# Placing the weight looks by the one plan, and storing the last output tile in two transfers

## The chip, the cores and the metric

The kernel runs on one core of one Trainium2 chip. The metric is the time of one execution on the device in microseconds (us). TensorE multiplies matrices and leaves sums in PSUM banks of 128 partitions by 512 float32. VectorE and ScalarE read those banks and write to on-chip memory (SBUF). GpSimd makes masks. SyncE issues the transfers (DMA). Each engine works through its own instruction list in order and waits on semaphores for the others.

## The reference

Attention with a decaying state (per head 48 wide, 4 batches, 8 heads, 768 steps) is followed by a feed-forward block with two up-projections whose results are multiplied.

```python
f = 1.0 / (1.0 + np.exp(-f_logit))
for t in range(S):
    state = f[:, :, t, :, None] * state + np.einsum('bhd,bhe->bhde', k[:, :, t], v[:, :, t])
    y[:, :, t] = np.einsum('bhd,bhde->bhe', q[:, :, t], state)
x = y.transpose(0, 2, 1, 3).reshape(B * S, H * D)   # 3072 x 384
a = x @ w1                                          # 384 x 1024
b = x @ w2
h = a * b @ w3                                      # 1024 x 1024
out = h @ w_out                                     # 1024 x 384
```

The activations are float32. The weights arrive as float64 and are read as pairs of 32-bit words.

## The kernel before

The sequence is cut into 24 chunks of 128 steps. Chunks are worked through by an attention part (the scans of the gates, the products inside a chunk, the state). Four chunks make a block of 512 tokens, and there are six blocks, 0 to 5. The matrices w3 and w_out are first multiplied into one (the array `wc`), so a block needs an up part (w1, w2), the product of the two, and a down part (`wc`).

The up part of block 0 is plain. Blocks 1 and 2 use a scheme with seven products per pair of column tiles (`seven`, products at L990, copies at L1031 and L1034). Blocks 3, 4 and 5 use a scheme of 20 products per group (`many`, two groups g per block). Its products are listed in `CHAINS`. Each chain stays in one PSUM bank: a product adds to what the chain has there (`product`, L1145), and where the partial sum is wanted, ScalarE copies it out before the next product of the chain adds to it (`keep_`, L1166). VectorE makes sums of such copies and banks (L1189, from `Y_SUMS`) and multiplies halves of them into `ab` (L1201, L1208). The down part uses seven products as well (`down`): TensorE at L894 (the helper `three`), copies on ScalarE at L1262 and L1275, sums on VectorE at L1255 to L1306, the output tiles `o1` and `o2`, and one store of 128 x 384 for each (L1311).

After the attention is over, the 8 PSUM banks are all used by products. `bank()` gives them out: four are tiles of their own (`f`), and the other four are the two halves of the tile `pa` and the two halves of the tile `py`.

The order of all this is made by a planner in the kernel (`Plan`). Each piece of work is a task with an engine, an assumed cost, the tasks it depends on, and a priority. The planner repeatedly takes the task that can start earliest, and among equals the one with the lowest priority number, and so writes out one list, in which the instructions are then recorded. The recording adds the waits, from the tiles that each instruction reads and writes.

The looks are a check on the weights' range. All 34 pieces of w1, w2, w3 and w_out are read once more (512 KB each, `load`, L1544), and ScalarE passes over the high words of each twice: once for the sum of magnitudes (L1548), once for a count of signs (L1552). Each pass also reads out an accumulator. VectorE forms a verdict from them (`verdict`, L1560 to L1564), `judge` joins it with a check of the gates, `told` and `heard` (L1586, L1590) bring the 128 values onto one partition through DRAM, and `decided` (L1595, L1596) sets `left`, by which every engine branches at the very end to a general version or past it. The last product of the last block (`m3`, `final`) has the decision among its dependencies.

Before the change, the looks are placed in two rounds. `order` first plans everything with the looks taken off ScalarE (`listed`), notes where ScalarE is then idle for longer than `GAP`, and gives each pass the first such idle stretch from `FILL_FROM` on that holds it, not sooner than `RELOAD` after the look two places earlier. A second planning then uses these times as earliest starts, with a high priority. The looks' data go in turn to three buffers: the two halves of the tile `A` and a part of `place`.

Of the kernel before, what the change touches and what calls it, by code (L numbers as in the profile page):

```python
# [36 lines left out]
F32 = mybir.dt.float32  # L37
I32 = mybir.dt.int32
U32 = mybir.dt.uint32
# [6 lines left out]
P = 128  # L46
# [5 lines left out]
DM = H * D  # L52
# [3 lines left out]
TB = 512  # L56
# [29 lines left out]
HEAVY = 3  # L86
WITH_POOL = 0.6
LOOKS = 0.0
GAP = 0.2
FILL_FROM = 262.0  # L90
RELOAD = 6.0
SPREAD = 10.0
QLATE = 0.1
MANY = 3
W_LATE = 30
# [25 lines left out]
NWT = 15  # L121
# [5 lines left out]
class Plan:  # L127
# [13 lines left out]

        self.pools[name] = [None] * n

    def add(self, eng, cost, emit, deps=(), prio=0.0, takes=(), frees=(), lag=0.2, slack=0.0, since=0.0, shared=False, gap=None):


        t = {
            "eng": eng, "cost": cost, "emit": emit, "deps": [d for d in deps if d is not None], "prio": prio,
            "takes": list(takes), "frees": list(frees), "lag": lag, "slack": slack, "since": since, "shared": shared, "at": None, "end": None, "no": len(self.tasks), "gap": gap,
        }  # L150
        self.tasks.append(t)
        return t

    def order(self):

        fill = [t for t in self.tasks if t["gap"] is not None]
        if fill:
            was = [(t["eng"], t["cost"]) for t in fill]
            for t in fill:
                t["eng"], t["cost"] = "none", 0.0  # L160
            slots, pools = ({n: (c, list(x)) for n, (c, x) in self.slots.items()}, {n: list(x) for n, x in self.pools.items()})
            busy = sorted((t["at"], t["end"]) for t in self.listed() if t["eng"] == "ACT" and t["cost"])
            for t in self.tasks:
                t["at"] = t["end"] = None
                t.pop("got", None)
            self.slots = {n: [c, x] for n, (c, x) in slots.items()}
            self.pools = pools
            for t, (t["eng"], t["cost"]) in zip(fill, was):
                pass
            gaps = [[a[1], b[0]] for a, b in zip(busy, busy[1:] + [(1e9, 1e9)]) if b[0] - a[1] > GAP]  # L170
            at = {}
            for t in fill:
                low = max([FILL_FROM] + [at[g] + w for g, w in t["gap"] if g in at])
                for g in gaps:
                    a = max(g[0], low)
                    if g[1] - a >= t["cost"] + GAP:
                        break
                t["since"], at[t["no"]], g[0] = a, a + t["cost"], a + t["cost"]
        return self.listed()

    def listed(self):
        free, done, left = dict.fromkeys(("PE", "DVE", "ACT", "POOL", "SP"), BEGIN), [], list(self.tasks)
        enders, masking = {}, []
        for t in self.tasks:
# [107 lines left out]
def ranged(ctx, tc, q, k, f_logit, v, w1, w2, w3, w_out, out, ident, w12, wc, left):  # L292
# [66 lines left out]
    def home(i):  # L359

        if i not in found:
            found[i] = homes[i]()
        return found[i]

    plan = Plan()
    plan.pool("f", NF)
    plan.pool("t", len(homes) - NWT + 4)
    plan.slot("a", 1)
    plan.slot("lane", 8)
    plan.slot("heavy", HEAVY)  # L370
# [13 lines left out]
    def temporary(i):  # L384

        if i < 2:
            return firsts[i]
        if i < 4:
            return ups[("u2", "u3")[i - 2]]
        return home(NWT + i - 4)  # L390

    def idle(n):

# [505 lines left out]
    def ffn(n):  # L899
# [325 lines left out]
        def down(i):  # L1225
# [79 lines left out]
            def c12():  # L1305
                nc.vector.tensor_tensor(q["o1"][:, DH:DM], q["Z"], dns["u2"], ALU.add)  # L1306

            def store(half):
                def emit():
                    t0 = n * TB + (i + half * UB // 2) * P  # L1310
                    nc.sync.dma_start(out[t0 : t0 + P], q["o1" if half == 0 else "o2"])  # L1311
                return emit

            n0 = 100 * n + 90 + i + 60 * (n > 1) + 30 * (n == NB - 2)
# [28 lines left out]
            pe("m3", m3, [q["c22"], q["S3"], q["m4"]] + ([judged] if final else []), -4)  # L1343
            dve("c12", 0.36, c12, [q["m3"], q["c11"]], frees=[q["m5"]])
            for half, deps in ((1, ("c21", "c22")), (0, ("c11", "c12"))):
                stores.append(moves(1, 197, 300, store(half), [q[nm] for nm in deps], -10))
            return q

# [183 lines left out]
    def ranges():  # L1532

        seen = [w[kc * P : kc * P + P] for w in (w1, w2) for kc in range(KM)] + [w3[jc] for jc in range(KF)]
        seen.append(w_out.rearrange("(p a) c -> p (a c)", a=KF))
        seen = [w[:, c : c + LOOK] for w in seen for c in range(0, w.shape[1], LOOK)]
        n = len(seen)
        sums_, counts, small = (spare[:, a : a + m] for a, m in ((0, n), (64, n), (128, 1)))
        words = [t.bitcast(U32) for t in (*flat, at(12864, WIDE))]
        his = [t.rearrange("p (n two) -> p n two", two=2)[:, :, 1].bitcast(F32) for t in words]  # L1540
        last = [plan.add("DVE", 0.1, lambda: nc.vector.memset(small, -SMALL), [tk[NU - 1][nm] for nm in ("r", "v", "mid")] + [tk[NU - 2]["v"]], -20)]

        def load(i):
            return lambda: nc.sync.dma_start(words[i % 3], seen[i].bitcast(U32))  # L1544

        def total(i):
            a = his[i % 3]
            return lambda: nc.scalar.activation(a, a, AF.Abs, accum_out=sums_[:, i : i + 1])  # L1548

        def count(i):  # L1550
            a = his[i % 3]
            return lambda: nc.scalar.activation(a, a, AF.Sign, bias=small, accum_out=counts[:, i : i + 1])  # L1552

        for i in range(n):
            ld = moves(1, LOOK, 400, load(i), last[:1] + [q["m3"] for q in blk[1]["seven"]] if i < 3 else last[i - 2 : i - 1], 500 + i, SURE_W, since=LOOKS)
            a = plan.add("ACT", 0.92, total(i), [ld], -400 + i, gap=[(last[-1]["no"], 0.0)] + ([(last[i - 2]["no"], RELOAD)] if i > 2 else []))
            last.append(plan.add("ACT", 0.95, count(i), [a], -400 + i, gap=[(a["no"], 0.0)]))

        def verdict():
            nc.vector.tensor_scalar(sums_, sums_, LARGE, None, ALU.is_le)  # L1560
            nc.vector.tensor_scalar(counts, counts, LOOK - 0.5, None, ALU.is_ge)
            nc.vector.tensor_tensor(sums_, sums_, counts, ALU.mult)
            where["weights"] = small
            nc.vector.tensor_reduce(out=small, in_=sums_, axis=AX.X, op=ALU.min)  # L1564

        return plan.add("DVE", 0.5, verdict, last, -20)
# [32 lines left out]
    for u in range(NU):  # L1599
# [13 lines left out]
        if u == NU - 1:  # L1613
            late = plan.add("none", 0.0, lambda: None)
            plan.pools["f"] += [late] * 4
            for nm in ("y", "mid", "m", "v"):
                tk[u][nm]["frees"].append(late)
            over["deps"] += [tk[u][nm] for nm in ("z", "v", "mid", "k", "q", "y")] + [tk[u - 1]["z"]]
            weighed = [ranges()] if wide else []
            looked = plan.add("DVE", 1.0, judge, [tk[i]["y"] for i in range(NU)] + weighed, -20)  # L1620
            sent = moves(1, 0.4, 250, told, [looked], 0, SPREAD)
            judged = plan.add("DVE", 0.2, decided, [moves(1, 0.4, 250, heard, [sent], 0, SPREAD)], -20)
        if u % UB == UB - 1:
            ffn(u // UB)
    first, last = {}, {}
# [396 lines left out]
```

## Time and profile before

| | |
|---|---|
| median of 3 runs | 464.53 us (464.53 to 465.14) |
| the profiled execution | 464.53 us |
| its span, first to last instruction | 462.8 us |
| TensorE busy | 454.1 us |
| VectorE busy | 364.8 us |
| ScalarE busy | 208.2 us |
| GpSimd busy | 64.7 us |
| mean granted TensorE clock | 0.998 |
| first look / end of the last one | 263.6 / 428.5 us |
| moved by DMA | 68.75 MB |

The shares are averages over the span; a matmul's end is modelled, so TensorE's busy time contains short waits between matmuls of one product. In a row of the timeline the columns are the start, the length, the engine, the line, the operation, the tiles (written <- read), the shapes, and how many instructions were joined; in square brackets stands the idle time of the engine before it and what ended it. PEld is TensorE's loading of weights. Each matmul of the program is recorded as two rows.

### The profile page before, as it was taken

The numbers are of one execution on the slowest core, as the hardware profiler recorded it, in microseconds if no ns is written. First come the engines' busy times: TensorE is split into PE (matmuls) and PEld (weight loads), VectorE is DVE, ScalarE is ACT, GpSimd is POOL, SyncE is SP. The second block draws the span as 40 slices with busy tenths as digits, with TensorE's granted clock in tenths as the row PEclk, the third lists the DMA queues.
The fourth block names the chain that finished last, engine by engine and source line by source line (L and its number), as shares of the span: only waits on it lengthen the run. The fifth ranks groups of instructions, "written<-read, shape, count | busy, mean of one in ns | idle before, by whom it ended". The sixth has DMA issues, their size and how long they took to land.

```text
span 462.8 us, 11767 instructions
## 1 busy us (share of the span) xinstructions
PE 454.1 (98%) x4800; PEld 395.6 (85%) x4800; DVE 364.8 (79%) x657; ACT 208.2 (45%) x468; POOL 64.7 (14%) x90
## 2 busy tenths in 40 slices
PE   8999999999999999999999999999999999999995
PEld 6778885666899888889998889998889988889995
DVE  8998999999898999989983598894669377767641
ACT  4565344532234444442432356664654666675000
POOL 9330001121122332322322000000000000000000
PEclk9999999999999999999999999999999999999999
DMA  6899899743246764445424335634135623330111
GB/s 181 269 297 306 268 343 276 260 103 87 80 110 192 205 186 113 133 135 166 120 57 113 111 112 178 221 113 149 47 124 176 200 91 92 90 95 0 35 68 40
DMA packets 43165, 68.75 MB, mean 149 GB/s; under 512 B 5201, under 2 KB 28242, under 8 KB 42082
## 3 DMA queue, kind: packets, MB, share of 16 engines
q1 hardware_dynamic: 43106, 67.95, 48.0%
q8 instruction: 39, 0.64, 0.6%
q14 instruction: 20, 0.16, 0.1%
HBM read 58.88 MB, written 9.04 MB: 147 GB/s over the span
## 4 chain that ended last, share of the span: by engine, by line
PE 93%; POOL 2%; DVE 2%; issue 1%; ACT 0%; POOLq 0%; DVEq 0%
PE f L894 26%; PE f L990 14%; PE f L1145 10%; PE f L1477 9%; PE pa L1145 7%; PE py L1145 5%; PE py L894 3%; PE py L650 3%; PE pa L894 3%; PE pa L576 2%; PE pa L683 2%; PE f L590 2%; PE py L669 2%; PE pa L990 1%; POOL ab L434 1%; PE f L396 1%
## 5 line engine op out<-in xcount | busy, mean ns | idle before, releaser
L706 POOL TENSOR_SCALAR_AFFINE_SELECT A<-A 64x512 f32<-64x512 f32 (+1 forms) x46 | 43.4, 943 | 104.0 <-ACT A L700 101.9
L1477 PE MATMUL f<-place 128*128 128x384 f32 x128 | 42.7, 488 | 0.0
L894 PE MATMUL f<-xt,w 128*128 128x256 f32 x192 | 42.1, 380 | 0.0
L894 PEld LDWEIGHTS f<-xt,w 128*128 128x128 f32 x192 | 36.3, 190 | 5.0
L894 PE MATMUL f<-place 128*128 128x192 f32 x216 | 39.5, 328 | 0.0
L1477 PEld LDWEIGHTS f<-place 128*128 128x128 f32 x128 | 23.8, 190 | 15.3
L894 PEld LDWEIGHTS f<-place 128*128 128x128 f32 x216 | 35.4, 190 | 0.5 <-issue 0.2
L990 PE MATMUL f<-xt,w 128*128 128x256 f32 x132 | 34.2, 379 | 0.0
L545 DVE TENSOR_TENSOR_SCAN bwd<-gate,back 112x512 f32<-112x512 f32 x24 | 30.8, 1285 | 0.7
L523 DVE TENSOR_TENSOR_SCAN fwd<-gate,floor 112x512 f32<-112x512 f32 x24 | 30.5, 1271 | 1.1 <-ACT gate L515 0.3
L990 PEld LDWEIGHTS f<-xt,w 128*128 128x128 f32 x132 | 24.8, 190 | 3.1
L842 ACT ACTIVATE ys<-py 112x512 f32<-112x512 f32 x22 | 13.1, 596 | 28.2 <-PE py L669 28.2
L1415 ACT ACTIVATE place<-place 128x512 f32<-128x512 uint32 (+2 forms) x24 | 21.1, 890 | 10.1 <-DMA place<-in_w_dram 7.9
L894 PE MATMUL f<-wc,ab 128*128 128x192 f32 x128 | 23.4, 326 | 0.0
L990 PE MATMUL f<-place 128*128 128x256 f32 x84 | 22.4, 385 | 0.0
L806 POOL TENSOR_TENSOR G<-lasts,gate 112x4 f32<-112x4 f32 x20 | 10.7, 535 | 81.3 <-ACT lasts L528 50.3
L894 PEld LDWEIGHTS f<-wc,ab 128*128 128x128 f32 x128 | 21.4, 190 | 0.4
L515 ACT ACTIVATE gate<-f 112x512 f32<-112x512 f32 x22 | 13.9, 632 | 15.4 <-DVE bwd L545 6.6
L650 PEld LDWEIGHTS py<-A,vt 64*64 64x64 f32 (+1 forms) x672 | 13.3, 127 | 7.3 <-issue 5.6
L650 PE MATMUL py<-A,vt 64*64 64x64 f32 (+1 forms) x672 | 18.1, 223 | 0.2
L1552 ACT ACTIVATE A<-A,back 128x512 f32<-128x512 f32 x23 | 17.9, 778 | 0.3
L990 PEld LDWEIGHTS f<-place 128*128 128x128 f32 x84 | 15.3, 190 | 2.2 <-ACT place L1031 0.2
(345 smaller groups left out, 1046.4 us busy)
## 6 DMA issues: line engine op xcount, KB each, us to landing
place<-in_w_dram SPq DMA_DIRECT2D x21, 512.0 KB, 6.4
A<-in_w_dram SPq DMA_DIRECT2D x19, 512.0 KB, 4.0
place<-in_w_dram SPq DMA_DIRECT2D x8, 1024.0 KB, 6.9
out_dram<-o SPq DMA_DIRECT2D x24, 192.0 KB, 2.3
q<-in_q_dram SPq DMA_DIRECT2D x46, 96.0 KB, 3.0
vt<-in_v_dram SPq DMA_DIRECT2D x23, 192.0 KB, 3.2
k<-in_k_dram SPq DMA_DIRECT2D x44, 96.0 KB, 2.5
yt<-ys SPq DMA_DIRECT2D x44, 96.0 KB, 2.9
```

Of the source, the lines that this page charges most:

```text
L515: nc.scalar.activation(gate[u % 2][:, 0:NQ], fu, AF.Sigmoid)
L523: nc.vector.tensor_tensor_scan(s["P"], gate[u % 2][:, 0:NQ], floor, 0.0, ALU.mult, ALU.max)
L545: nc.vector.tensor_tensor_scan(s["R"][:, ::-1], gate[u % 2][:, NQ:0:-1], back[:, ::-1], 0.0, ALU.mult, ALU.max)
L650: done = nc.tensor.matmul(y_block(u, hp, par, half)[p0 : p0 + w], lhsT=s["v"][half * W : half * W + W, h * D : h * D + w], rhs=s["A"][half ...
L706: nc.gpsimd.affine_select(out=a, in_=a, pattern=pattern, compare_op=ALU.is_ge, fill=0.0, base=0, channel_multiplier=-1,)
L842: nc.scalar.activation(ys, py, AF.Copy, accum_out=ysum[:, u : u + 1])
L894: nc.tensor.matmul(out_, lhsT=lhs[i], rhs=rhs[i], start=start and i == 0, stop=i == len(lhs) - 1, skip_group_check=True,)
L990: nc.tensor.matmul(q[nm][:, which * TH : which * TH + TH], lhsT=lhs[i](which), rhs=rhs[i], start=start and which == 0 and i == 0, stop=i = ...
L1145: nc.tensor.matmul(banks[g, c][:, which * TH : which * TH + TH], lhsT=lhs, rhs=x_node(a), start=first and which == 0, stop=True, skip_grou ...
L1415: nc.scalar.activation(lo.bitcast(F32), lo, AF.Copy, bias=2.0, scale=2.0**-51)
L1477: nc.tensor.matmul(w3s["p", jc], lhsT=w3s[jc][:, kc * P : kc * P + P], rhs=wos[:, kc], start=(kc == 0), stop=(kc == KF - 1),)
L1552: return lambda: nc.scalar.activation(a, a, AF.Sign, bias=small, accum_out=counts[:, i : i + 1])
```

## The change

The second round of planning goes away: `gap`, `order`'s first part and the constants `GAP`, `FILL_FROM` and `RELOAD` are removed, and `listed` becomes `order`. The passes of a look are ordinary tasks with priority 500 and up, the last of all. Their data go to two buffers, the halves of `A`; the third part of `place` becomes two more temporaries for the copies and sums of `many`. The assumed extra time of the round trip through DRAM goes from 10 to 20. The last output tile `o1` of the last block is stored in two transfers of 192 columns, the first one when `c11` is done and the second one when `c12` is.

```diff
--- before.py
+++ after.py
@@ -86,10 +86,6 @@
 HEAVY = 3
 WITH_POOL = 0.6
 LOOKS = 0.0
-GAP = 0.2
-FILL_FROM = 262.0
-RELOAD = 6.0
-SPREAD = 10.0
 QLATE = 0.1
 MANY = 3
 W_LATE = 30
@@ -141,44 +137,17 @@
 
         self.pools[name] = [None] * n
 
-    def add(self, eng, cost, emit, deps=(), prio=0.0, takes=(), frees=(), lag=0.2, slack=0.0, since=0.0, shared=False, gap=None):
+    def add(self, eng, cost, emit, deps=(), prio=0.0, takes=(), frees=(), lag=0.2, slack=0.0, since=0.0, shared=False):
 
 
         t = {
             "eng": eng, "cost": cost, "emit": emit, "deps": [d for d in deps if d is not None], "prio": prio,
-            "takes": list(takes), "frees": list(frees), "lag": lag, "slack": slack, "since": since, "shared": shared, "at": None, "end": None, "no": len(self.tasks), "gap": gap,
+            "takes": list(takes), "frees": list(frees), "lag": lag, "slack": slack, "since": since, "shared": shared, "at": None, "end": None, "no": len(self.tasks),
         }
         self.tasks.append(t)
         return t
 
     def order(self):
-
-        fill = [t for t in self.tasks if t["gap"] is not None]
-        if fill:
-            was = [(t["eng"], t["cost"]) for t in fill]
-            for t in fill:
-                t["eng"], t["cost"] = "none", 0.0
-            slots, pools = ({n: (c, list(x)) for n, (c, x) in self.slots.items()}, {n: list(x) for n, x in self.pools.items()})
-            busy = sorted((t["at"], t["end"]) for t in self.listed() if t["eng"] == "ACT" and t["cost"])
-            for t in self.tasks:
-                t["at"] = t["end"] = None
-                t.pop("got", None)
-            self.slots = {n: [c, x] for n, (c, x) in slots.items()}
-            self.pools = pools
-            for t, (t["eng"], t["cost"]) in zip(fill, was):
-                pass
-            gaps = [[a[1], b[0]] for a, b in zip(busy, busy[1:] + [(1e9, 1e9)]) if b[0] - a[1] > GAP]
-            at = {}
-            for t in fill:
-                low = max([FILL_FROM] + [at[g] + w for g, w in t["gap"] if g in at])
-                for g in gaps:
-                    a = max(g[0], low)
-                    if g[1] - a >= t["cost"] + GAP:
-                        break
-                t["since"], at[t["no"]], g[0] = a, a + t["cost"], a + t["cost"]
-        return self.listed()
-
-    def listed(self):
         free, done, left = dict.fromkeys(("PE", "DVE", "ACT", "POOL", "SP"), BEGIN), [], list(self.tasks)
         enders, masking = {}, []
         for t in self.tasks:
@@ -364,7 +333,7 @@
 
     plan = Plan()
     plan.pool("f", NF)
-    plan.pool("t", len(homes) - NWT + 4)
+    plan.pool("t", len(homes) - NWT + 6)
     plan.slot("a", 1)
     plan.slot("lane", 8)
     plan.slot("heavy", HEAVY)
@@ -387,7 +356,7 @@
             return firsts[i]
         if i < 4:
             return ups[("u2", "u3")[i - 2]]
-        return home(NWT + i - 4)
+        return at(12864 + TB * (i - 4), TB) if i < 6 else home(NWT + i - 6)
 
     def idle(n):
 
@@ -1305,10 +1274,10 @@
             def c12():
                 nc.vector.tensor_tensor(q["o1"][:, DH:DM], q["Z"], dns["u2"], ALU.add)
 
-            def store(half):
+            def store(half, c0=0, c1=DM):
                 def emit():
                     t0 = n * TB + (i + half * UB // 2) * P
-                    nc.sync.dma_start(out[t0 : t0 + P], q["o1" if half == 0 else "o2"])
+                    nc.sync.dma_start(out[t0 : t0 + P, c0:c1], q["o1" if half == 0 else "o2"][:, c0:c1])
                 return emit
 
             n0 = 100 * n + 90 + i + 60 * (n > 1) + 30 * (n == NB - 2)
@@ -1343,6 +1312,10 @@
             pe("m3", m3, [q["c22"], q["S3"], q["m4"]] + ([judged] if final else []), -4)
             dve("c12", 0.36, c12, [q["m3"], q["c11"]], frees=[q["m5"]])
             for half, deps in ((1, ("c21", "c22")), (0, ("c11", "c12"))):
+                if final and half == 0:
+                    stores.append(moves(1, 98, 300, store(0, 0, DH), [q["c11"]], -10))
+                    stores.append(moves(1, 98, 300, store(0, DH, DM), [q["c12"]], -10))
+                    continue
                 stores.append(moves(1, 197, 300, store(half), [q[nm] for nm in deps], -10))
             return q
 
@@ -1536,25 +1509,25 @@
         seen = [w[:, c : c + LOOK] for w in seen for c in range(0, w.shape[1], LOOK)]
         n = len(seen)
         sums_, counts, small = (spare[:, a : a + m] for a, m in ((0, n), (64, n), (128, 1)))
-        words = [t.bitcast(U32) for t in (*flat, at(12864, WIDE))]
-        his = [t.rearrange("p (n two) -> p n two", two=2)[:, :, 1].bitcast(F32) for t in words]
+        words = both.bitcast(U32)
+        hi = words.rearrange("p (n two) -> p n two", two=2)[:, :, 1].bitcast(F32)
         last = [plan.add("DVE", 0.1, lambda: nc.vector.memset(small, -SMALL), [tk[NU - 1][nm] for nm in ("r", "v", "mid")] + [tk[NU - 2]["v"]], -20)]
 
         def load(i):
-            return lambda: nc.sync.dma_start(words[i % 3], seen[i].bitcast(U32))
+            return lambda: nc.sync.dma_start(words[:, i % 2 * WIDE : (i % 2 + 1) * WIDE], seen[i].bitcast(U32))
 
         def total(i):
-            a = his[i % 3]
+            a = hi[:, i % 2 * LOOK : (i % 2 + 1) * LOOK]
             return lambda: nc.scalar.activation(a, a, AF.Abs, accum_out=sums_[:, i : i + 1])
 
         def count(i):
-            a = his[i % 3]
+            a = hi[:, i % 2 * LOOK : (i % 2 + 1) * LOOK]
             return lambda: nc.scalar.activation(a, a, AF.Sign, bias=small, accum_out=counts[:, i : i + 1])
 
         for i in range(n):
-            ld = moves(1, LOOK, 400, load(i), last[:1] + [q["m3"] for q in blk[1]["seven"]] if i < 3 else last[i - 2 : i - 1], 500 + i, SURE_W, since=LOOKS)
-            a = plan.add("ACT", 0.92, total(i), [ld], -400 + i, gap=[(last[-1]["no"], 0.0)] + ([(last[i - 2]["no"], RELOAD)] if i > 2 else []))
-            last.append(plan.add("ACT", 0.95, count(i), [a], -400 + i, gap=[(a["no"], 0.0)]))
+            ld = moves(1, LOOK, 400, load(i), last[:1] if i < 2 else last[i - 1 : i], 500 + i, SURE_W, since=LOOKS)
+            a = plan.add("ACT", 0.92, total(i), [ld], 500 + i)
+            last.append(plan.add("ACT", 0.95, count(i), [a], 500 + i))
 
         def verdict():
             nc.vector.tensor_scalar(sums_, sums_, LARGE, None, ALU.is_le)
@@ -1618,8 +1591,8 @@
             over["deps"] += [tk[u][nm] for nm in ("z", "v", "mid", "k", "q", "y")] + [tk[u - 1]["z"]]
             weighed = [ranges()] if wide else []
             looked = plan.add("DVE", 1.0, judge, [tk[i]["y"] for i in range(NU)] + weighed, -20)
-            sent = moves(1, 0.4, 250, told, [looked], 0, SPREAD)
-            judged = plan.add("DVE", 0.2, decided, [moves(1, 0.4, 250, heard, [sent], 0, SPREAD)], -20)
+            sent = moves(1, 0.4, 250, told, [looked], 0, 20.0)
+            judged = plan.add("DVE", 0.2, decided, [moves(1, 0.4, 250, heard, [sent], 0, 20.0)], -20)
         if u % UB == UB - 1:
             ffn(u // UB)
     first, last = {}, {}
```

## The prediction

> **What bounds the kernel now.** I read the page's engine shares and its chain first, then the busy time by stretch, then the chip's own order around the few stalls, then the end.
>
> ```profile
> PE 454.1 (98%) x4800; PEld 395.6 (85%) x4800; DVE 364.8 (79%) x657; ACT 208.2 (45%) x468; POOL 64.7 (14%) x90
> PE 93%; POOL 2%; DVE 2%; issue 1%; ACT 0%; POOLq 0%; DVEq 0%
> ```
>
> TensorE is busy for 98% of the span and is 93% of the chain that ended last. So nothing that runs beside it counts until TensorE has to wait. The next view is the busy time in stretches (us, then busy time and instructions of PE, PEld, DVE, ACT, POOL).
>
> ```profile
> 255.00:341.00 86.00, 85.70 (x430) 76.64 (x423) 64.08 (x126) 47.21 (x111) 0.00 (x0) 1.00 0.41 133
> 341.00:428.00 87.00, 86.94 (x441) 78.90 (x439) 59.96 (x116) 54.86 (x126) 0.00 (x0) 1.00 0.34 108
> ```
>
> The looks run from 263.6 to 428.5 us, in just these stretches. TensorE has almost no idle time left there, while ScalarE works for about 0.6 of it. The clock column is 1.00. The timeline shows the one large stall (start, length, engine, line):
>
> ```profile
> 335.86 1.03 PE L1145 MATMUL pa<-xt,w 128*128 128x256 f32 x4
> 336.72 1.03 PE L1145 MATMUL py<-xt,w 128*128 128x256 f32 x4
> 336.92 0.59 ACT L1166 COPY place<-pa 128x512 f32<-128x512 f32 x1 [1.32 <-PE pa L1145]
> 337.41 0.59 ACT L1166 COPY ys<-pa 128x512 f32<-128x512 f32 x1
> 338.05 0.73 PEld L1145 LDWEIGHTS pa<-xt,K 128*128 128x128 f32 x4 [0.70 <-ACT ys L1166]
> 338.05 1.13 PE L1145 MATMUL pa<-xt,K 128*128 128x256 f32 x4 [0.30 <-ACT ys L1166]
> ```
>
> Four rows are one product; its slot is 336.72-335.86 = 0.86. The product in pa at 338.05 should have begun at 337.58 and came 0.46 late. It continues the chain whose copy is the first one (place<-pa, over at 337.51), yet it starts only 0.05 after the second copy, which reads the *other* half of the tile pa. So two banks of one tile wait for each other in this program. By the same reckoning (distance between starts less the usual slot) I find in the trace from 277 us: 0.17 at 306.6-306.9, 0.08 at 323.0, 0.08 at 335.2, 0.56 at 338.0 (0.46 plus 0.10 behind it), 0.08 at 382.5, 0.33 at 427.9. Sum 1.30. That is all that a better plan could win from TensorE.
>
> A look hides like this:
>
> ```profile
> 340.35 0.68 ACT L1548 ACTIVATE A<-A 128x512 f32<-128x512 f32 x1
> 340.93 0.19 ACT L1548 ACTIVATION_READ_ACCUMULATOR A<-A 128x1 f32 x1
> 341.02 0.57 ACT L1166 COPY ys<-py 128x512 f32<-128x512 f32 x1
> ```
>
> A first pass holds ScalarE for 341.02-340.35 = 0.67; the second one, by 344.62 to 345.37, for 0.75. The end of the span:
>
> ```profile
> 456.78 1.31 PE pa L894 x8
> 458.10 0.02 issue
> 458.12 0.36 DVE o L1306
> DMA to landing us min/median/max: 2.7/2.7/2.7
> ```
>
> The last line answers for the last store alone: issued at 458.54, it lands at 461.27, and SyncE's closing waits follow to 462.80. The profiled execution took 464.53: 1.73 lie around the span. It is also the median shown, so the sum below starts from 464.53.
>
> **The change, part by part.**
>
> *The number of instructions* is the same on TensorE, VectorE and ScalarE; SyncE issues one DMA more. Nothing is saved in work: 34 looks are two passes each, before and after. So the sum is made of stalls and of the end.
>
> *The looks' places.* They now have the last priority in the one plan instead of places in the gaps of a plan without them. As the plan takes what can start earliest, a look goes in whenever ScalarE is free, and the copy that becomes ready a moment later waits behind it. Moved along with them: every load of a look on SyncE's queue (34, past xt gathers and stores), the verdict, and from 306 us on the order of the products and sums. I went through the changed program's order product by product and asked what each waits for and what stands before that on its engine. TensorE's steps and the copies keep their slots from the rows above. Three places exceed their cover.
>
> A. Block 4, second group, chain 1. ScalarE's order there is:
>
> ```
> TensorCopy Q<-pa 128x512 [waits PE]
> Activation A,back<-A 128x512        (a look's first pass)
> TensorCopy ys<-pa 128x512
> ```
>
> Both copies wait for the same product, since they read the two halves of pa. TensorE has one product in bank f for cover (0.86) and then one in pa, which waits for ys<-pa. From the end of the slot: 0.24 until ScalarE begins (copy L1262 at 441.26, slot end 441.02), a copy's slot 0.49 (337.41-336.92), the pass 0.67, the copy 0.59, 0.05 to restart: 2.04-0.86 = 1.2 lost. Without the look 0.5 would be lost. Bounds 0 (neither copy waits for the other half's product) and 1.3.
>
> B. Block 5's first two products, both of chain 0 in one half of py, with no copy between them in the source. The second nevertheless waits for ScalarE: the copy Q<-py of the *other* half was recorded between the two, so it waits for the first product and the second product waits for it. Nothing covers it: 0.24+0.59+0.05 = 0.9. No look is in this one; it is the plan's luck, as in the row at 338.05. Bounds 0 (the wait is on another copy, already over) and 1.0.
>
> C. Block 5, chain 5, into py: it waits for a VectorE sum, which waits for a copy behind a look. Nearest row: 0.33 at 427.9, also TensorE waiting for VectorE. I take 0.3, bounds 0 and 0.5.
>
> Small waits like the three of 0.08: 0.1 (0 to 0.3). Sum 2.5, in place of 1.30, whose places are all ordered anew: **TensorE ends 1.2 later** (bounds 0-1.3 = -1.3 and 1.3+1.0+0.5+0.3-1.3 = +1.8).
>
> On one point a page speaks against A and B. The Trainium skill, "PSUM — Partial Sum Buffer", section "PSUM bank collisions raise a hardware error", asks for semaphores by bank, and finds different banks free of collisions; by it neither product needs to wait for the other half, and the sum would lose A and B, 2.1 us. The row at 338.05 shows this program waiting all the same, and the row decides.
>
> *Two buffers instead of three for the looks.* Loads land in 3.4/3.9/5.3 us (min/median/max). In the changed order only the other look's two passes (1.4) and a few copies stand between a pass that frees a buffer and the pass that wants the new data, so ScalarE will wait for data, up to 2.5 us (3.9-1.4), with copies queued behind. The three places where this is largest are in the block boundaries' output products, where the next copy has idle time before it now: 1.79 at 295.5, 3.17 at 353.5, 2.19 at 366.0. I take 0; the cover ends when loads take over 6 us.
>
> *The two temporaries more, and the spread of 20 for the verdict's round trip.* They act through the order, counted above. The verdict is formed 37 VectorE instructions earlier. SyncE then stands still for the round trip (the word told lands in 8.8 us), and the stores queued behind it are those of the closing output products, whose tiles are made later than that. The answer was no wait before either (0.26 at 455.80 right behind a sum, the last product on its beat at 456.62). 0.
>
> *The last store in two.* The first 192 columns (copied by ScalarE at 452.92) leave several us early. The last store carries 96 KB. Quiet 192 KB stores land in 1.8/1.9, this one in 2.73, so it is held up by 0.9 by other traffic at the end. Half of its packets: 8 of 65 ns on each of 16 engines is 0.52, half of it 0.26. Against that, 96 KB writes of yt land in 2.0 at best, no faster. Bounds: 0 and 0.9; I take 0.25, since the end's other traffic stays. The extra issue (0.33) lies on SyncE's idle time.
>
> Sum: 464.53+1.2-0.25 = **465.5**.
>
> **The rivals.** *Neither half waits for the other* (or the waited copies are long over): A and B at 0, C 0.3, small ones 0.1, so 0.4-1.3 = -0.9, and the store -0.25: 463.4, faster. For it: I read the waits from the order, no row shows these two. Against: the row at 338.05. It decides when A and B together fall below 0.2. *The end eats it*: stalls as forecast, but the last store lands like a quiet one, -0.9: 464.8, no change. For it: 2.73 against 1.85. Against: the instruction fetches at the end remain. *Late data*: one or two loads of a look over 6 us hold copies for 1 to 3 us: 466.5 to 468.5, slower. For it: the missing third buffer; a fetch of 6.1 us stands in the trace at 435. Against: the longest load was 5.3.
>
> **How the numbers follow.** A measurement here tells about 0.2% from no change, 0.93 us: slower means above 465.46, faster below 463.60. The likeliest case (0.60) has its own range 464.9 to 466.1; its middle lies at the bound, so I give 0.33 of it to slower, 0.25 to same, 0.02 to faster. Neither half waits: 0.11 (0.09 faster, 0.02 same). The end eats it: 0.13, same. Late data: 0.16, slower. Slower 0.33+0.16 = 0.49, same 0.25+0.02+0.13 = 0.40, faster 0.02+0.09 = 0.11. For 8 in 10 the range goes from 464.2 to 466.9: below it lies most of the faster case, above it half of late data.
>
> **What would show it.** Right: two TensorE gaps of about 1.2 and 0.9 before products in pa and py (line 1114 there), the first with a look between two copies; the last matmul 1.2 later; last store landing in 2.2 to 2.6. Wrong: gaps elsewhere on DMA landings of looks, or none; the end shortened by over 0.6.

## The result, and the profile after

The changed kernel takes 466.03 us (median of 22 runs), and the kernel before, measured beside it, 464.72 (22 runs): ratio 1.0025, with a 95% interval of 1.0015 to 1.0035. It is slower by 1.3 us. The bound of 0.2% between "slower" and "no change" lies inside the interval. The profiled execution took 465.47, where the sum of the prediction was 465.5; its span is 463.74 (462.80 before).

The page of the changed kernel, engine shares and the chain that ended last:

```profile
PE 454.4 (98%) x4800; PEld 395.7 (85%) x4800; DVE 364.6 (79%) x657; ACT 206.6 (45%) x468; POOL 64.9 (14%) x90
PE 95%; DVE 2%; DMA 1%; SPq 1%; ACT 1%; issue 0%; DVEq 0%; ACTq 0%
```

TensorE is the bound as before. The busy time by stretch, in the columns of the prediction's second view (stretch, length, then busy us and instructions of PE, PEld, DVE, ACT, POOL, clock, DMA share, GB/s), says where its time went:

```profile
255.00:341.00 86.00, 86.00 (x426) 77.54 (x427) 65.39 (x128) 52.45 (x126) 0.00 (x0) 1.00 0.46 146
341.00:428.00 87.00, 85.39 (x428) 76.65 (x427) 58.74 (x123) 48.41 (x109) 0.00 (x0) 1.00 0.31 96
```

The first stretch has lost its idle 0.30 and the second one has gained: 87.00-85.39 = 1.61 idle, where it was 0.06 (the waits below sum to more, since a matmul's modelled end covers part of each). ScalarE's work has moved the other way, 5.2 us more in the first stretch and 6.5 less in the second, because the looks now end at 402.8 and not at 428.5. So TensorE stands still more in a stretch in which ScalarE does less. The three places in the timeline (start, length, engine, line, operation, tiles, and in brackets the idle time before it):

```profile
372.17 0.59 ACT L1135 COPY Q<-pa 128x512 f32<-128x512 f32 x1 [1.14 <-PE pa L1114]
372.65 0.66 ACT L1521 ACTIVATE A<-A 128x512 f32<-128x512 f32 x1
373.20 0.19 ACT L1521 ACTIVATION_READ_ACCUMULATOR A<-A 128x1 f32 x1
373.30 0.57 ACT L1135 COPY ys<-pa 128x512 f32<-128x512 f32 x1
373.93 1.13 PE L1114 MATMUL pa<-xt,q 128*128 128x256 f32 x4 [0.94 <-ACT ys L1135]
...
383.73 0.58 ACT L1135 COPY Q<-py 128x512 f32<-128x512 f32 x1 [2.20 <-PE py L1114]
384.37 1.13 PE L1114 MATMUL py<-xt,w 128*128 128x256 f32 x4 [0.68 <-ACT Q L1135]
...
402.07 0.69 DVE L1158 TENSOR_TENSOR ys<-ys,py 128x512 f32<-128x512 f32 x1 [0.41 <-ACT Q L1135]
402.81 1.13 PE L1114 MATMUL py<-place,floor 128*128 128x256 f32 x4
```

The first five rows are A: a copy of pa, a look's first pass, the second copy of pa, and the product into pa 0.06 after that copy's end. The next two are B, a product into py that starts 0.06 after a copy of py. The last two are C, behind a VectorE sum that reads py. Reckoned as in the prediction (distance between the starts of two matmul rows less the usual slot), A is 1.20, B 0.94, C 0.23. From 277 us all waits come to 2.78, against 1.31 before. The last matmul starts at 459.01 (457.76 before), and the last store, of 96 KB now, lands 2.5 us after its issue at 459.76:

```profile
DMA to landing us min/median/max: 2.5/2.5/2.5
```

One wait was not in the prediction, 0.24 at 358.9. Its source stands three microseconds ahead of it on VectorE:

```profile
355.56 0.69 DVE L1158 TENSOR_TENSOR ys<-place,pa 128x512 f32<-128x512 f32 x1 [1.85 <-PE pa L863]
```

A sum that reads one half of pa waits 1.85 us for a product of the output part (L863). Its successors on VectorE are late with it, and the last of them, L1237, holds up TensorE.

### The profile page after: what moved, and what is told of

The parts are those of the page before. It is cut to its first block, busy times and chain, and to the rows that moved or that the text cites. A ratio compares the mean times of both kernels' runs of the same rounds, so it can differ in the third digit from the quotient of the medians.

```text
span 463.7 us, 11765 instructions
## 1 busy us (share of the span) xinstructions
PE 454.4 (98%) x4800; PEld 395.7 (85%) x4800; DVE 364.6 (79%) x657; ACT 206.6 (45%) x468; POOL 64.9 (14%) x90
## 4 chain that ended last, share of the span: by engine, by line
PE 95%; DVE 2%; DMA 1%; SPq 1%; ACT 1%; issue 0%; DVEq 0%; ACTq 0%
PE f L863 25%; PE f L959 14%; PE f L1114 12%; PE f L1450 9%; PE pa L1114 5%; PE py L1114 5%; PE py L863 5%; PE pa L863 3%; PE py L619 3%; PE pa L545 2%; PE pa L652 2%; PE f L559 2%; PE py L638 2%; PE pa L959 1%; PE f L365 1%; PE py L959 1%
## 5 line engine op out<-in xcount | busy, mean ns | idle before, releaser
L863 PE MATMUL f<-xt,w 128*128 128x256 f32 x192 | 42.1, 380 | 0.0
L863 PEld LDWEIGHTS f<-xt,w 128*128 128x128 f32 x192 | 36.3, 190 | 5.0
L1450 PEld LDWEIGHTS f<-place 128*128 128x128 f32 x128 | 23.8, 190 | 15.3
L863 PE MATMUL f<-place 128*128 128x192 f32 x184 | 33.9, 329 | 0.0
L863 PEld LDWEIGHTS f<-place 128*128 128x128 f32 x184 | 30.1, 190 | 0.8 <-DVE place L1237 0.3
L1525 ACT ACTIVATE A<-A,back 128x512 f32<-128x512 f32 x34 | 26.6, 782 | 0.5
L1521 ACT ACTIVATE A<-A 128x512 f32<-128x512 f32 x34 | 23.3, 684 | 4.1 <-DMA A<-in_w_dram 4.1
L863 PE MATMUL f<-wc,ab 128*128 128x192 f32 x128 | 23.4, 326 | 0.0
L775 POOL TENSOR_TENSOR G<-lasts,gate 112x4 f32<-112x4 f32 x20 | 10.7, 533 | 81.3 <-ACT lasts L497 49.5
L863 PEld LDWEIGHTS f<-wc,ab 128*128 128x128 f32 x128 | 21.3, 190 | 0.3
```

The costliest lines, as they stand in the source:

```text
L863: nc.tensor.matmul(out_, lhsT=lhs[i], rhs=rhs[i], start=start and i == 0, stop=i == len(lhs) - 1, skip_group_check=True,)
L1450: nc.tensor.matmul(w3s["p", jc], lhsT=w3s[jc][:, kc * P : kc * P + P], rhs=wos[:, kc], start=(kc == 0), stop=(kc == KF - 1),)
```

## The experiments

The theory: the plan's new order meets waits between the two halves of pa and of py, which the recording sets because the halves are one tile; a look lengthens such a wait where it stands between two copies. The rivals: the looks themselves, in ScalarE's way, are the cause; the data from two buffers are late; the split store is worth nothing or much more than 0.25.

In the table, "waits" is the sum of TensorE's waits from 277 us in the profiled execution, "end" is the time from the start of the last matmul to the end of the span, and the ratio is to the kernel before, run on the same chip.

| kernel | waits | end | median, us | ratio (95% interval) |
|---|---|---|---|---|
| before | 1.31 | 5.04 | 464.72 | |
| after | 2.78 | 4.73 | 466.03 | 1.0025 (1.0015 to 1.0035) |
| after_banks | 0.00 | 4.87 | 463.03 | 0.9976 (0.9961 to 0.9991) |
| after_py_halves | 1.52 | 4.73 | 463.94 | 0.9997 (0.9988 to 1.0007) |
| after_nopasses | 1.99 | 4.46 | 464.62 | 1.0006 (0.9997 to 1.0015) |
| after_three | 6.19 | 4.57 | 469.00 | 1.0108 (1.0092 to 1.0123) |
| after_three_banks | 0.00 | 4.77 | 462.71 | 0.9963 (0.9950 to 0.9977) |
| before_split | 1.31 | 4.66 | 463.74 | 0.9992 (0.9983 to 1.0001) |
| after_onestore | 2.77 | 4.82 | 465.70 | 1.0035 (1.0021 to 1.0048) |
| before_banks_split | 0.00 | 4.60 | 462.83 | 0.9973 (0.9964 to 0.9983) |
| before_two | 1.40 | 15.37 | 474.99 | 1.0228 (1.0214 to 1.0242) |
| before_two_r4 | 1.90 | 6.11 | 466.01 | 1.0036 (1.0022 to 1.0050) |

The kernel before ran at 464.26 to 464.39 beside the experiments, 0.3 to 0.5 below the 464.72 beside the changed kernel, so medians are compared through the ratios.

**The four halves as tiles of their own.** Once the attention is over, its PSUM tiles are given back (their pool, now the last one opened, is closed) and four tiles of one bank each take their place. The order of the instructions on TensorE, VectorE, ScalarE and SyncE is that of the changed kernel, row by row.

```diff
-            nm = ("pa", "py")[(plan.got - NF) // 2]
-            if nm not in found:
-                found[nm] = ps.tile([P, 2, NQ], F32, name=nm)
-            return found[nm][:, plan.got % 2]
+            if "late" not in found:
+                early_ps.close()
+                found["late"] = ctx.enter_context(tc.tile_pool(name="ps_l", bufs=1, space=PSUM))
+            return found["late"].tile([P, TB], F32, name=f"l{plan.got - NF}")
```

> The changed kernel with the same order of instructions on every engine; only the halves of pa and py are four tiles of their own once the attention is over, so that a product in one half no longer waits for a reader of the other half. Theory (waits between two halves of one tile, dealt out by the plan's order): the TensorE waits A (1.20 at 373.9), B (0.94 at 384.4) and C (0.23 at 402.8) vanish together with the small ones; their sum from 277 us falls from 2.77 to under 0.4, and the time to 463.4 (463.0 to 463.9), below the kernel before. Rival (ScalarE is late for the product's own bank, because looks stand in its way): A and C stay, the sum stays above 1.3, the time above 465.2. Rival (a wait removed comes back in the next reader, VectorE or ScalarE): the sum falls but the time by less than 1 us, above 465.0.

Measured: no TensorE wait of over 0.04 us from 277 us on, 463.03 us. The same five instructions as in A, the tiles now called l:

```profile
371.12 0.59 ACT L1135 COPY Q<-l 128x512 f32<-128x512 f32 x1 [0.28 <-PE l L1114]
371.61 0.69 ACT L1521 ACTIVATE A<-A 128x512 f32<-128x512 f32 x1
372.18 0.19 ACT L1521 ACTIVATION_READ_ACCUMULATOR A<-A 128x1 f32 x1
372.27 0.57 ACT L1135 COPY ys<-l 128x512 f32<-128x512 f32 x1
372.65 1.03 PE L1114 MATMUL l<-xt,q 128*128 128x256 f32 x4
```

The look stands where it stood, and the product starts 0.19 before the second copy is over (372.27+0.57 = 372.84). The copies are early too: Q<-l begins at 371.12, while the second of two products is still running (they run from 370.06 to 371.95; in the changed kernel the copy began after both, at 372.17, and had waited 1.14). The unforeseen wait has the same cause, since that VectorE sum no longer waits for the output product and is over a microsecond and a half sooner:

```profile
353.69 0.68 DVE L1158 TENSOR_TENSOR ys<-place,l 128x512 f32<-128x512 f32 x1
```

So all of A, B, C and the small ones were waits between halves, and this is shown with no instruction moved. Late data are no part of it: in this run, too, ScalarE waits up to 2.3 us for the load of a look, and TensorE waits for nothing.

**Only the halves of py.** The same, but pa stays one tile.

```diff
+                found["pa"] = found["late"].tile([P, 2, NQ], F32, name="pa")
-            return found["late"].tile([P, TB], F32, name=f"l{plan.got - NF}")
+            return found["pa"][:, plan.got % 2] if plan.got < NF + 2 else found["late"].tile([P, TB], F32, name=f"l{plan.got - NF}")
```

> The changed kernel, same order, with only the two halves of py as tiles of their own after the attention; pa stays one tile of two halves. Theory (each wait belongs to the other half of its own tile): B (0.94 at 384.4), C (0.23) and the 0.08 at 387 go, A (1.20 at 373.9) stays, with the 0.24 at 358.9, whose late VectorE sum reads pa; sum from 277 us 2.78-1.25 = 1.5, time 1.25 below the changed kernel and 1.4 above the one with all four halves apart, 464.4 (464.0 to 464.9), ratio to before 1.000. Rival (the waits hang together: B's copy is late because A came before it): A alone pulls the others along, sum above 2.2.

Measured: waits 1.52, ratio 0.9997. A stays to the hundredth (0.10 of its 1.20 lies, as before, on the row behind it), B is gone:

```profile
373.81 0.70 PE L1115 MATMUL pa<-xt,q 128*128 128x256 f32 x2 [0.93 <-ACT ys L1136]
...
382.76 1.67 PE L1115 MATMUL l<-xt,w 128*128 128x256 f32 x7
```

The four halves together are worth 2.78 us of waits, py's alone 1.26. The times follow: (0.9997-0.9976) x 464.3 = 1.0 us lie between this kernel and the one with all four apart, for 1.52 of waits; the intervals of the two ratios allow that.

**The looks' passes taken off ScalarE.** Loads and order stay; both passes of every look are left out, and the verdict on the weights is a constant.

```diff
-            return lambda: nc.scalar.activation(a, a, AF.Abs, accum_out=sums_[:, i : i + 1])
+            return lambda: None
...
-            return lambda: nc.scalar.activation(a, a, AF.Sign, bias=small, accum_out=counts[:, i : i + 1])
+            return lambda: None
```

> The changed kernel without the looks' passes over the data on ScalarE (all 34 loads stay; the verdict on the weights is formed from a constant, so the weights' range is not looked at). The order of what is left is the same. Theory (the order's luck with waits between halves, looks only lengthen A and C): A falls from 1.20 to 0.5, B stays at 0.9, C goes; sum from 277 us 1.6 to 1.8, time 465.1 (464.8 to 465.5), not below the kernel before. Rival (looks in ScalarE's way are the cause of the loss): A, B and C go, sum under 0.6, time 463.8 or less.

```profile
372.37 0.59 ACT L1135 COPY Q<-pa 128x512 f32<-128x512 f32 x1 [1.14 <-PE pa L1114]
372.85 0.59 ACT L1135 COPY ys<-pa 128x512 f32<-128x512 f32 x1
373.50 0.91 PE L1114 MATMUL pa<-xt,q 128*128 128x256 f32 x3 [0.30 <-ACT ys L1135]
```

A is 0.56 without its look, B 0.99, C gone; waits 1.99, above the 1.6 to 1.8 expected, since the 0.24 at 358.9 and two small ones stay. The ratio 1.0006 is no gain over the kernel before, though ScalarE works 48 us less (158.5 busy). The looks as such are 0.8 of the 2.78; the order is the rest. The median of 464.62 lies 0.18 below the stated 464.8 to 465.5, which started from a kernel before at 464.7; here it ran at 464.39.

**Three buffers for the looks again, in the one plan.**

```diff
-    plan.pool("t", len(homes) - NWT + 6)
+    plan.pool("t", len(homes) - NWT + 4)
...
-        words = both.bitcast(U32)
+        words = [t.bitcast(U32) for t in (*flat, at(12864, WIDE))]
...
-            ld = moves(1, LOOK, 400, load(i), last[:1] if i < 2 else last[i - 1 : i], 500 + i, SURE_W, since=LOOKS)
+            ld = moves(1, LOOK, 400, load(i), last[:1] + [q["m3"] for q in blk[1]["seven"]] if i < 3 else last[i - 2 : i - 1], 500 + i, SURE_W, since=LOOKS)
```

> The changed kernel with the looks' data in three buffers again (and the two temporaries more taken away with them); the looks stay in the one plan, the last store in two. The plan then writes out another order of products. Read from that order, seven products from the first look on wait for a reader of the other half of their tile: one behind a look (1.2, as A), one with no cover (0.9, as B), two behind a copy (0.5 each, as the row before the change), three in the output products and their neighbours (0.4 to 0.7 each). Theory (the order's luck): sum of TensorE waits about 5 (3.5 to 5.5), time 3.5 above before, 467.9 (466.5 to 468.5). Rival (the loss comes from the two buffers: data late, copies held): three buffers undo it, sum of waits under 2, time 464.4 to 465.0.

Measured: waits 6.19, 469.00 us, more than the 3.5 to 5.5 that I read from the order. Undoing a part of the change made it worse by four microseconds: the plan writes out a third order, with more meetings of halves. Two of them:

```profile
378.08 0.42 DVE L1177 TENSOR_TENSOR ab<-pa,ab 128x256 f32<-128x256 f32 x1
378.55 1.13 PE L1114 MATMUL pa<-place,q 128*128 128x256 f32 x4 [0.87 <-DVE ab L1177]
...
427.51 0.59 ACT L1135 COPY place<-py 128x512 f32<-128x512 f32 x1 [1.84 <-PE py L863]
428.15 1.13 PE L1114 MATMUL py<-place,k 128*128 128x256 f32 x4 [0.68 <-ACT place L1135]
```

The largest, 1.13, has no look at all: a copy, a half copy and a VectorE product of the other half of pa stand before it.

**The same with tiles of their own.** The edit is that of the first experiment.

> The same kernel as the one with three buffers, the same order on every engine, with the halves of pa and py as four tiles of their own after the attention. Theory: all waits from the first look on go (sum under 0.4), the time is 463.0 (462.6 to 463.6), the same as the changed kernel with tiles of their own, though the two orders differed by some 2.5 us before. Rival (part of the loss is looks or copies that come late for their own bank): the sum stays above 1.5, the time above 464.5.

Measured: waits 0.00, 462.71 us. The product of the row at 378.55 starts here at 374.64 and waits for nothing:

```profile
374.38 0.42 DVE L1177 TENSOR_TENSOR ab<-l,ab 128x256 f32<-128x256 f32 x1
374.64 1.03 PE L1114 MATMUL l<-place,q 128*128 128x256 f32 x4
```

Two orders that stood 3.9 us apart by their ratios (1.0108 and 1.0025) come out so close that no difference can be told, with intervals that overlap (0.9950 to 0.9977 and 0.9961 to 0.9991).

**The store alone, and the change without it.** In the first of these the kernel before gets the split store and nothing else, and in the second one the changed kernel loses it. No other engine's order moves in either.

```diff
+                if final and half == 0:
+                    stores.append(moves(1, 98, 300, store(0, 0, DH), [q["c11"]], -10))
+                    stores.append(moves(1, 98, 300, store(0, DH, DM), [q["c12"]], -10))
+                    continue
                 stores.append(moves(1, 197, 300, store(half), [q[nm] for nm in deps], -10))
```

> The kernel before with one thing more: the last output tile stored in two transfers of 192 columns. The order of all engines but SyncE's stores is that of the kernel before. Theory (the end's other traffic stays, half of the packets are saved): the last transfer lands 2.5 us after its issue in place of 2.73, the time is 464.5, ratio 0.9995. Rival (the last transfer lands like a quiet one): 1.8 to 1.9 after its issue, 463.8, ratio 0.998. Rival (the split does nothing): 2.7, 464.7.

> The changed kernel with the last tile stored in one transfer again; nothing else differs in any engine's order. Theory: the TensorE waits stay as they are (sum 2.8 from 277 us), the last transfer lands 2.7 us after its issue in place of 2.5, the time is 466.3, ratio to before 1.003. Rival (the split is worth the whole 0.9): 466.9. Rival (worth nothing): 466.0, landing 2.5.

Measured: on the kernel before, the last transfer lands in 2.4 with the split (2.7 without), ratio 0.9992 (0.9995 expected). The changed kernel without the split has the ratio 1.0035 (1.003 expected). The landing of its last transfer is not in the trace: the store issued at 457.59, the last but one, lands in 2.8, and the last one, issued at 458.93, has no landing on record. What is on record are the data packets. On the kernel before, the last one ends 2.25 us after the last issue without the split and 1.82 with it; on the changed kernel it ends at 1.92 without and 1.90 with it. So one pair shows a gain and the other one shows none. Over all the runs here whose verdict comes early, the end is 4.46 to 4.87 with the split (eight profiles, mean 4.67) and 5.04 and 4.82 without (mean 4.93). The means differ by 0.26, but the two groups overlap and the interval of before_split still holds no gain. A gain of about a quarter of a microsecond fits, and so does a smaller one or none. A gain of 0.9 does not: the last 96 KB land in 2.2 at the soonest, the first 96 KB of the same tile, stored 5 us earlier, in 1.6. The size stays open.

**The order before with tiles of its own and the split store.** Both edits, on the kernel before.

> The kernel before with the halves of pa and py as tiles of their own after the attention, and the last tile stored in two transfers; the order is that of the kernel before. Theory: its waits of 1.3 go, 0.25 at the end, 464.4-1.3-0.25 = 462.9 (462.5 to 463.5); with the waits between halves gone, the one plan and the plan with gaps come out alike (within 0.4 of the changed kernel with tiles of its own, 463.0). Rival (the gaps are worth something by themselves): 0.5 or more below that one.

Measured: waits 0.00, 462.83 us. This, after_banks and after_three_banks beat both kernels of the change, by 1.1 to 1.7 us against the kernel before, and no difference between the three can be told. With the waits between halves gone, it makes no difference that can be told which of these three ways the looks are put. The page of after_banks:

```profile
PE 453.1 (98%) x4800; PEld 396.2 (86%) x4800; DVE 365.0 (79%) x657; ACT 207.8 (45%) x468; POOL 64.8 (14%) x90
```

**Two buffers in the kernel before.** The looks keep their places in gaps, with two buffers and the two temporaries more. A look may come no sooner than 6 us (`RELOAD`) after the pass that frees its buffer. With three buffers that is the look three places earlier and not two: `last` begins with the memset, so `last[i - 2]` is the count of look i-3. With two buffers it is the look two places earlier (`last[i - 1]`).

```diff
-        words = [t.bitcast(U32) for t in (*flat, at(12864, WIDE))]
+        words = [t.bitcast(U32) for t in flat]
...
-            a = plan.add("ACT", 0.92, total(i), [ld], -400 + i, gap=[(last[-1]["no"], 0.0)] + ([(last[i - 2]["no"], RELOAD)] if i > 2 else []))
+            a = plan.add("ACT", 0.92, total(i), [ld], -400 + i, gap=[(last[-1]["no"], 0.0)] + ([(last[i - 1]["no"], RELOAD)] if i > 1 else []))
```

> The kernel before with the looks' data in two buffers and the two temporaries more; the looks stay where the plan without them left gaps, one load sooner to wait for. TensorE's order is that of the kernel before. Theory (two buffers cost nothing by themselves): TensorE's waits stay at 1.3, ratio 1.000, 464.4 (464.0 to 464.8). Rival (late data holds ScalarE and the copies behind it): waits of 1 us and more appear where a copy stands behind a look that waits for its load, time above 465.3.

Measured: 474.99 us, a clear miss. TensorE did as expected (waits 1.40, last matmul at 457.89), but the end grew from 5.04 to 15.37. The last pass of a look, and the rows of SyncE and VectorE around the end:

```profile
453.14 0.76 ACT L1552 ACTIVATE A<-A,back 128x512 f32<-128x512 f32 x1
456.34 0.33 SPq L1586 DMA_DIRECT2D good<-good  x1
463.65 0.30 SPq L1590 DMA_DIRECT2D row<-good  x1
466.70 0.27 DVE L1595 TENSOR_REDUCE least<-row 1x1 f32<-1x128 f32 x1 [9.51 <-DMA row<-good]
467.81 0.36 DVE L1306 TENSOR_TENSOR o<-pa,place 128x192 f32<-128x192 f32 x1 [0.67 <-DVE left L1596]
468.24 0.36 SPq L1311 DMA_DIRECT2D out_dram<-o  x1
```

With two buffers each pair of looks takes at least 6 us plus its passes, so the last pass ends at 454.0 in place of 428.5. The verdict goes out at 456.34, comes back 7.3+3.0 us later, and the last output sum is queued behind it on VectorE. I had asked only what the loads would hold up, and not when the last look would be over.

**The same with a spacing of 4 us.**

```diff
-RELOAD = 6.0
+RELOAD = 4.0
```

> The kernel before with two buffers, as in the run that took 474.99, but a look may come 4 us in place of 6 after the pass that frees its buffer; so the looks can be done some 25 us sooner. Theory (that run lost its time because the gaps' spacing of 6 us with two buffers put the last look at 454, and the verdict's round trip of 7.3 and 3.0 us behind it stood on the end): the last look is over by 432, the last product's start to the end of the span is 5.0 again (15.4 there), TensorE's waits are 1.2 to 1.8, the time is 464.6 (464.1 to 465.4). Rival (two buffers bring the data late, whatever the spacing): loads of 4 to 5 us hold ScalarE and the copies behind it, waits above 2.5, time above 466.

Measured: 466.01 us, above the stated range. The cause of the run before is confirmed (last look over at 430.0, the end back from 15.37 to 6.11), but two things were missed. The waits are 1.90, where the order of products had moved once more; and the decision still falls on the end, at 457.81, as the chain's last pieces show (DVEq is VectorE's own queue, L1303 its reading of the decision):

```profile
457.99 0.66 DVEq L1303
458.81 0.36 DVE o L1306
```

VectorE reads the decision before its last sum, so the last store is issued 1.06 after the start of the last matmul (0.78 before), and it lands in 3.5 us and not in 2.7. The decision is this late by VectorE's order: the transfer back was issued at 441.1, and VectorE did not wait for it. The time is the one that the rival gave (above 466), its cause is not there: ScalarE's longest wait for a look's load is 2.5, as it is in the changed kernel, and its waits for looks' data end at 286.5 to 350.6, while the TensorE waits that the kernel before did not have stand at 372.7, 388.6 and 402.0. What sets these three was not tested.

## Why the prediction was right

**The bound and the sum.** The waits went up by 1.47 (forecast 1.2), TensorE's end by 1.25, the end gave back 5.04-4.73 = 0.31 (forecast 0.25), and the span grew by 0.94. The forecast of TensorE's end was met because two misses cancel: the waits are 0.27 larger than summed, and what lies before 277 us was 0.22 shorter in this profile, which was no step of mine. That the profiled execution met the sum to 0.03 is luck too: the median is 466.03, and the forecast difference of 0.95 us stands against 1.31 between the medians, inside the 0.7 to 1.6 of the ratio's interval.

**A, B and C.** Predicted 1.2, 0.9 and 0.3, measured 1.20, 0.94 and 0.23, at the named products. The part of A without its look was put at 0.5 and measured 0.56. For C the text named the look and the VectorE sum but not that this sum reads py, the other half again, which the runs with py's halves apart show.

**Small ones.** Put at 0.1 (0 to 0.3), measured 0.16 for the two of 0.08, plus the 0.24 at 358.9. That step failed in its reasoning: I followed only products that wait for a reader of the other half. Readers also wait for a product in the other half, as the 1.85 on VectorE shows, and pass it on. The bound covered the small ones or this one, and was too narrow for both.

**Neither half waits for the other.** The Trainium skill, "PSUM — Partial Sum Buffer", section "PSUM bank collisions raise a hardware error", finds accesses to different banks free of collisions, and by it A and B would have been nothing. The row at 338.05 was the better guide for this kernel, in which the recording waits by the tile. In after_banks, with each bank a tile of its own, the products do run beside the readers of other banks, as the page has it: the waits go from 2.78 to 0.00.

**Two buffers: 0.** Right for this change: ScalarE waited for loads up to 2.5 us as forecast, no TensorE wait lies behind them, and all recorded landings of looks came within 5.1. But the 0 did not follow from the text's own rows: the 2.5 is more than the 1.79 that it named as cover at 295.5. The rows show why it held:

```profile
291.23 0.69 ACT L1521 ACTIVATE A<-A 128x512 f32<-128x512 f32 x1 [2.53 <-DMA A<-in_w_dram]
295.31 0.59 ACT L1135 COPY place<-f 128x512 f32<-128x512 f32 x1 [1.75 <-PE f L1114]
```

The longest wait stands here, and the next copy still finds ScalarE idle for 1.75 before it, since three passes stand between the copies at this place where five stood before. The 0 rested on the end, too: the one plan ends the looks at 402.8, 56 us ahead of the last matmul. The text gave the verdict's earlier place 0, which is right, but did not say that two buffers are harmless only as long as the last look ends early; before_two has the same buffers with the last look over at 454.0, and is 10.7 us slower.

**The last store: 0.25.** 2.73 to 2.51 at the landing, 0.31 at the end, in one pair of profiles; as the runs of the store alone leave its size open, meeting it this closely is partly luck. The step to it was misread: the split does not halve the packets. The last store is 128 packets in both kernels, of 1536 bytes and 66 ns (median) before and of 768 bytes and 39 ns after, so 8 packets on each of 16 engines are shorter by 8 x 0.027 = 0.22 us, near the 0.26 of the text. Two instruction fetches of 8 KB start between its issue and its landing in both profiles (0.72 and 0.57 us before, 0.53 and 0.42 after); that they are what holds it up is not shown.

**The chances.** Slower had 0.49, no change 0.40; the result of 0.25% lies on the bound between them, where the likeliest case was put.

## What to carry to other kernels

When a plan hands out halves of a tile as if they were independent buffers, see from one row whether the program waits by the tile, and if so count the meetings in the new order, in both directions: a writer behind a reader of the other half, and a reader behind a writer of it. Making each buffer a tile of its own took away 1.3 to 6.2 us of waits here without moving an instruction, which is more than any of the three orders differ by afterwards. And for work that is moved off the bound, ask not only what it holds up on its way but when its last piece ends, and what stands behind that on the last engine.

## What the runs showed that was not expected

The same order of instructions up to 150 us starts its first product of the seven-product scheme at 150.33 in the profile of the kernel before, at 149.22 in that of before_split and at 150.52 in that of after_three_banks. A span of one profile can thus differ by a microsecond for reasons that lie far ahead of the change; the sums of waits (1.31 in both of the first two) do not. The distance is there by 84 us, where VectorE's 121st instruction starts at 83.96, 82.86 and 84.18, with a granted clock of 1.00 in all three. What causes it was not looked for.

Removing 48 us of work from ScalarE (after_nopasses) took no more off the changed kernel (1.0025 to 1.0006) than making tiles of the two halves of py did (1.0025 to 0.9997).
